# Decayed linear attention and a GELU MLP on one core: an earlier score block, a halved weight slice, and a shorter load lead

## The chip, the core and the metric

The kernel runs on one core of a Trainium2 chip. The metric is device time in microseconds (us) of one execution; for a comparison the medians of several executions are used. TensorE (PE) multiplies matrices, VectorE (DVE), ScalarE (ACT) and GpSimd (POOL) work elementwise, SyncE (SP) issues transfers. Each engine works through its own instructions in order and waits at semaphores for the others. GpSimd computes and also issues the loads that convert float32 to bf16.

## The reference

Inputs are q, k, v of 4 batches, 8 heads, 768 positions, 64 channels, a decay lam per head, and two weight matrices. Attention runs over blocks of positions with a state that decays:

```python
for b in range(nb):
    intra = np.einsum('bhic,bhjc->bhij', qb, kb) * Dmask[None]
    intra = np.einsum('bhij,bhjd->bhid', intra, vb)
    inter = np.einsum('bhid,bhde->bhie', qb * lam_pow[None], kv_state)
    out[:, :, sl] = intra + inter
    kb_dec = kb * rev_pow[None]
    kv_state = lam_block[None, :, None, None] * kv_state + np.einsum('bhsd,bhse->bhde', kb_dec, vb)
```

Its output, as 3072 rows of 512, goes through an MLP: h = x @ w_in (512 to 2048), g = h * (1 + erf(h / sqrt 2)) / 2, result = g @ w_out (2048 to 512), in float32.

## The kernel before

Positions are cut into 24 chunks of 128 (six for each batch), and four chunks make a group of 512 rows. Attention of a chunk gives a slice of x, transposed; when a group's x is full, its MLP follows: 16 column blocks of the first matmul (mm1, L288, each ended by a GELU on ScalarE, L290), then four output tiles of the second (mm2, L300).

One chunk's attention consists of these steps:

- begin: takes its loaded q, k, v.
- decay_k (L157): k scaled for the state, k_dec. On GpSimd, except in the first two chunks.
- transposes (L169): for chunks 0 to 7, on TensorE, emptied by ScalarE (kT) and VectorE (qT, with the decay). dma_transposes (L185): for chunks 8 to 23 both are transposes by transfers from SyncE; q is scaled on GpSimd first (q_hat, L190).
- scores (L193): eight matmuls into two PSUM tiles, two masking multiplications on VectorE. The PSUM tag has two buffers.
- next_state (L204): the product of k_dec and v is added to the state.
- outputs (L249): the state part (L253 or L259) and the score part (L263) in one PSUM tile o_ps, of which there is only one buffer; empty_outputs (L269) copies it to x, on ScalarE for chunks 0 to 7.

The order is written by hand and kept. The start (L371 to L397) interleaves chunks 0 to 3, with matmuls on an idle tile (keep_warm, L356) between them. GpSimd issues the loads of chunks 0 to 3 first (L76), then slice 0 of w_in (L381; a slice is a quarter of the columns, 512 of 2048), scales k of chunks 2 and 3, and then issues the other three slices of w_in, four slices of w_out (L399 to L402) and the loads of chunks 4 and on (L409 to L420). Transfers from GpSimd run on one queue in the order of issue. They use eight semaphores in turn, so that an issue waits until the eighth transfer before it has landed.

During the MLP of group 0, chunks 4 to 7 are worked in by a table of block numbers (group0, L425): at block 22 the transposes of chunk 4, and so on. Chunks 8 to 23 have due times: a list of steps sorted by the amount of matmul work done (L438 to L444), from which step (L446) is called between MLP blocks. A step of kind 0 begins chunk n: it issues kT's transfer on SyncE, q_hat on GpSimd, qT's transfer on SyncE, k_dec on GpSimd, and then, by prefetch (L342), all loads up to chunk n + 3 that are not issued yet. When chunk 8 begins, loads up to chunk 9 have been issued.

Of the kernel before, what the change touches and what calls it, by code (L numbers as in the profile page):

```python
# [15 lines left out]
def kernel(  # L16
# [10 lines left out]
    nc = tc.nc  # L27

    B, H, S, D = q.shape
    d_model, d_ff = moe_w_in.shape  # L30
# [9 lines left out]
    M = 4  # L40
# [22 lines left out]
    def load(n, name):  # L63
        raw[n, name] = qkv_pool.tile([128, H, D], BF16, tag=name, name=f"{name}_t")
        nc.gpsimd.dma_start(raw[n, name], chunk_of(name, n))  # L65
# [13 lines left out]
    w_in_t = w_pool.tile([128, NK1, d_ff], BF16)  # L79
    w_out_t = w_pool.tile([128, NK2, d_model], BF16)  # L80
    w_in_r = moe_w_in.rearrange("(ko ki) f -> ki ko f", ki=128)
    w_out_r = moe_w_out.rearrange("(ko ki) f -> ki ko f", ki=128)
    NS = 4

    def load_w_in(s):
        f = d_ff // NS
        nc.gpsimd.dma_start(w_in_t[:, :, s * f:(s + 1) * f], w_in_r[:, :, s * f:(s + 1) * f])

    def load_w_out(s):
        f = NK2 // NS  # L90
        nc.gpsimd.dma_start(w_out_t[:, s * f:(s + 1) * f, :], w_out_r[:, s * f:(s + 1) * f, :])
# [40 lines left out]
    def make_lam_blk():  # L132
        for hi in range(2):
            p = slice(hi * D, (hi + 1) * D)
            nc.vector.tensor_copy(lam_blk[p, :, p], lam_c_b[p])
# [9 lines left out]
    xT = {}  # L145
    states = {}

    def bank(shape, dtype, tag, name):
        return ps.tile(shape, dtype, tag=tag, name=name, bufs=2 if tag in ("sc", "mh", "mo") else 1)

    def begin(n, early=False):
        c = Chunk()
        c.n, c.sb, c.early = n, n % NB, early
        c.q, c.k, c.v = (raw.pop((n, name)) for name in "qkv")
        return c
# [29 lines left out]
    def dma_transposes(c):  # L185
        c.kT = work_pool.tile([128, HP, C], BF16, tag="kT", name="kT")
        c.qT = work_pool.tile([128, HP, C], BF16, tag="qT", name="qT")
        q_hat = work_pool.tile([128, H, D], BF16, tag="qh", name="q_hat")
        nc.sync.dma_start_transpose(out=c.kT, in_=c.k.rearrange("p h d -> p (h d)"))
        nc.gpsimd.tensor_mul(q_hat, c.q, lam_p[:, :, None].to_broadcast((128, H, D)))  # L190
        nc.sync.dma_start_transpose(out=c.qT, in_=q_hat.rearrange("p h d -> p (h d)"))

    def scores(c):  # L193
        sc_ps = [bank([128, HP, C], F32, "sc", f"sc_ps{hi}") for hi in range(2)]
        for hp in range(HP):
            for hi in range(2):
                p = slice(hi * D, (hi + 1) * D)
                nc.tensor.matmul(sc_ps[hi][:, hp, :], c.kT[p, hp, :], c.qT[p, hp, :], start=True, stop=True)  # L198
        c.sc_m = work_pool.tile([128, HP, 2, C], BF16, tag="sc_m", name="sc_m")
        dmask_r = dmask.rearrange("p (hp hi) i -> p hp hi i", hi=2)  # L200
        for hi in range(2):
            nc.vector.tensor_mul(c.sc_m[:, :, hi, :], sc_ps[hi], dmask_r[:, :, hi, :])  # L202

    def next_state(c):  # L204
        if c.sb == NB - 1:
            return
        if not c.early:
            return next_state_full(c)
        kv_ps = bank([128, HP, D], F32, "t", "kv_ps")
        for hp in range(HP):  # L210
            for hi in range(2):
                h = 2 * hp + hi
                nc.tensor.matmul(kv_ps[hi * D:(hi + 1) * D, hp, :], c.k_dec[:, h, :], c.v[:, h, :],
                                 start=True, stop=True)
        if c.n == M - 1:
            for hi in range(2):
                p = slice(hi * D, (hi + 1) * D)
                nc.vector.tensor_add(first_blk[p, :, p], kv_ps[p], states[c.n][1][p])
            states[c.n + 1] = first_blk, None
            return  # L220
        new = work_pool.tile([128, HP, D], BF16, tag="state", name="state")
        if c.sb == 0:
            nc.vector.tensor_copy(new, kv_ps)
        else:
            nc.vector.tensor_add(new, kv_ps, states[c.n][1])
        old = work_pool.tile([128, HP, D], F32, tag="old", name="old")
        states[c.n + 1] = new, old

    def decay_state(c):
        new, old = states[c.n + 1]  # L230
        for hp in range(HP):
            nc.scalar.activation(old[:, hp, :], new[:, hp, :], ACT.Copy, scale=lam_c[:, hp:hp + 1])

    def next_state_full(c):

        kv_ps = bank([128, HP, 128], F32, "t", "kv_ps")
        for hp in range(HP):
            nc.tensor.matmul(kv_ps[:, hp, :], c.k_dec[:, 2 * hp:2 * hp + 2, :], c.v[:, 2 * hp:2 * hp + 2, :],  # L238
                             start=True, stop=True)
        new = work_pool.tile([128, HP, 128], BF16, tag="state_f", name="state")  # L240
        if c.sb == 0:
            nc.vector.tensor_mul(new, kv_ps, lam_blk)
        else:
            tmp = work_pool.tile([128, HP, 128], F32, tag="tmp", name="tmp")
            nc.vector.tensor_add(tmp, kv_ps, states[c.n][0])  # L245
            nc.vector.tensor_mul(new, tmp, lam_blk)  # L246
        states[c.n + 1] = new, None

    def outputs(c, x_t, off, evacuate=True):  # L249
        o_ps = bank([128, HP, C], F32, "o", "o_ps")  # L250
        if c.sb > 0 and not c.early:
            for hp in range(HP):
                nc.tensor.matmul(o_ps[:, hp, :], states[c.n][0][:, hp, :], c.qT[:, hp, :],  # L253
                                 start=(hp == 0), stop=False, skip_group_check=True)
        elif c.sb > 0:
            for hp in range(HP):
                for hi in range(2):
                    p = slice(hi * D, (hi + 1) * D)
                    nc.tensor.matmul(o_ps[p, hp, :], states[c.n][0][p, hp, :], c.qT[p, hp, :],  # L259
                                     start=(hp == 0), stop=False, skip_group_check=True)  # L260
        for hp in range(HP):
            for hi in range(2):
                nc.tensor.matmul(o_ps[hi * D:(hi + 1) * D, hp, :], c.v[:, 2 * hp + hi, :], c.sc_m[:, hp, hi, :],  # L263
                                 start=(c.sb == 0 and hp == 0), stop=True, skip_group_check=True)
        c.x_o, c.o_ps = x_t[:, :, off * C:(off + 1) * C], o_ps
        if evacuate:
            empty_outputs(c)

    def empty_outputs(c):  # L269
        if c.n < 2 * M:  # L270
            nc.scalar.copy(c.x_o, c.o_ps)
        else:
            nc.vector.tensor_copy(c.x_o, c.o_ps)  # L273
# [68 lines left out]
    def prefetch(upto):  # L342
        while next_load[0] <= min(upto, NCH - 1):
            for name in "kqv":
                load(next_load[0], name)
            next_load[0] += 1
# [3 lines left out]
    live = {}  # L350
# [5 lines left out]
    def keep_warm(n, new=True):  # L356

        if new:
            idle_ps[0] = bank([128, 512], F32, "mo", "idle_ps")
        for _ in range(n):  # L360
            nc.tensor.matmul(idle_ps[0], idle[:, :128], idle, start=True, stop=True)  # L361

    def early(s, between=lambda: None):
        live[s] = begin(s, early=True)
        if s == 1:
            decay_k(live[s], nc.vector)
        transposes(live[s], between)
        if s != 1:
            decay_k(live[s], nc.scalar if s == 0 else nc.gpsimd)
# [9 lines left out]
    outputs(live[0], xT[0], 0, evacuate=False)  # L379
    scores(live[1])  # L380
    load_w_in(0)  # L381
    keep_warm(1)
    early(2)
# [1 line left out]
    next_state(live[1])  # L385
    scores(live[2])
    decay_state(live[1])
    outputs(live[1], xT[0], 1, evacuate=False)
    keep_warm(1)
    early(3)  # L390
    empty_outputs(live[1])
    next_state(live[2])
    outputs(live[2], xT[0], 2)
    scores(live[3])
    keep_warm(4)
    outputs(live[3], xT[0], 3)
    decay_state(live[2])  # L397
    make_lam_blk()
    for s in range(1, NS):  # L399
        load_w_in(s)  # L400
    for s in range(NS):
        load_w_out(s)  # L402
# [43 lines left out]
    def step(minus_kind, n):  # L446
        kind = -minus_kind
        g = n // M - 1
        if kind == 0:
            live[n] = begin(n)  # L450
            dma_transposes(live[n])
            decay_k(live[n], nc.gpsimd)
            prefetch(n + 3)
        elif kind == 2:
            scores(live[n])
            next_state(live[n])
        else:
            outputs(live[n], xT[g + 1], n % M)
# [46 lines left out]
```

## Time and profile before

| | |
|---|---|
| median of 5 runs | 217.72 us (217.07 to 219.0) |
| the profiled execution | 218.01 us, its span 216.2 us |
| TensorE busy | 204.9 us (95% of the span) |
| GpSimd busy | 105.3 us |
| first mm1 matmul starts | 19.50 us |
| transposes of chunk 4 (block 22 of group 0) | 38.87 us |
| scores of chunk 8, of chunk 9 | 56.46 us, 65.47 us |

All times in the profile are counted from the span's start. The page lists busy time by engine, the span in 40 slices, the chain of work that ended last, and groups of instructions with what ended the idle time before them. TensorE's idle time is 11.3 us in all: 1.2 before its first matmul, some 4 in the start up to 20 us, and pieces before single instructions later.

### The profile page before, as it was taken

The numbers are of one execution on the slowest core, as the hardware profiler recorded it, in microseconds if no ns is written. First come the engines' busy times: TensorE is split into PE (matmuls) and PEld (weight loads), VectorE is DVE, ScalarE is ACT, GpSimd is POOL, SyncE is SP. The second block draws the span as 40 slices with busy tenths as digits, with TensorE's granted clock in tenths as the row PEclk, the third lists the DMA queues.
The fourth block names the chain that finished last, engine by engine and source line by source line (L and its number), as shares of the span: only waits on it lengthen the run. The fifth ranks groups of instructions, "written<-read, shape, count | busy, mean of one in ns | idle before, by whom it ended". The sixth has DMA issues, their size and how long they took to land.

```text
span 216.2 us, 3545 instructions
## 1 busy us (share of the span) xinstructions
PE 204.9 (95%) x1422; PEld 102.9 (48%) x1446; DVE 73.4 (34%) x120; ACT 91.1 (42%) x169; POOL 105.3 (49%) x120
## 2 busy tenths in 40 slices
PE   7769999999998999999999999999999999999993
PEld 2345444555444545445545444545445545444452
DVE  4895000378515323406415413405415413100000
ACT  6975672334564221465221465221465221566121
POOL 8998333998999999467940819213000000000000
PEclk9999999999999999999999999999999999999999
DMA  6999999999999999999998697514351012100112
GB/s 40 146 158 195 200 207 185 155 209 137 189 142 125 165 147 163 200 125 96 112 125 150 78 164 64 36 69 127 75 98 24 3 70 75 50 0 3 49 49 97
DMA packets 100272, 24.35 MB, mean 113 GB/s; under 512 B 92960, under 2 KB 97312, under 8 KB 100256
## 3 DMA queue, kind: packets, MB, share of 16 engines
q0 software_dynamic: 79104, 13.64, 84.4%
q1 hardware_dynamic: 21152, 10.50, 22.7%
q8 instruction: 11, 0.18, 0.3%
q14 instruction: 5, 0.04, 0.1%
HBM read 27.27 MB, written 6.29 MB: 155 GB/s over the span
## 4 chain that ended last, share of the span: by engine, by line
PE 70%; DMA 14%; POOL 12%; issue 2%; ACT 0%; POOLq 0%
PE o_ps L300 32%; PE h_ps L288 28%; DMA q_t<-in_q_dram 8%; DMA w_in_t<-in_moe_w_in_dram 3%; POOL q_t L65 3%; POOL k_t L65 3%; POOL v_t L65 3%; DMA qT<-q_hat 3%; PE o_ps L263 3%; PE sc_ps L198 2%; POOL k_dec L167 2%; PE kv_ps L238 2%; PE o_ps L315 2%; PE o_ps L253 1%; POOL q_hat L190 1%
## 5 line engine op out<-in xcount | busy, mean ns | idle before, releaser
L288 PE MATMUL h_ps<-x_t,w_in_t 128*128 128x512 bf16 (+2 forms) x378 | 84.8, 377 | 1.0 <-DMA w_in_t<-in_moe_w_in_dram 0.5
L300 PE MATMUL o_ps<-w_out_t,g_t 128*128 128x512 bf16 x355 | 81.8, 379 | 0.8 <-issue 0.3
L290 ACT ACTIVATE g_t<-h_ps 128x512 bf16<-128x512 f32 x96 | 57.3, 597 | 33.9 <-PE h_ps L288 33.9
L288 PEld LDWEIGHTS <-w_in_t 128*128 128x128 bf16 x388 | 37.3, 98 | 43.8 <-DMA w_in_t<-in_moe_w_in_dram 0.6
L300 PEld LDWEIGHTS <-g_t 128*128 128x128 bf16 x368 | 34.7, 98 | 39.6
L305 ACT COPY o_sb<-o_ps 128x512 f32<-128x512 f32 x23 | 13.5, 586 | 68.3 <-PE o_ps L300 65.4
L273 DVE CAST x_t<-o_ps 128x512 bf16<-128x512 f32 x16 | 11.1, 692 | 73.0 <-PE o_ps L263 73.0
L202 DVE TENSOR_TENSOR sc_m<-sc_ps,dmask 128x512 bf16<-128x512 f32 x48 | 30.8, 683 | 14.7 <-PE sc_ps L198 14.4
L190 POOL TENSOR_TENSOR q_hat<-q_t,lam_p 128x512 bf16<-128x512 bf16 x16 | 16.9, 1057 | 18.1 <-DMA qT<-q_hat 17.3
L167 POOL TENSOR_TENSOR k_dec<-k_t,lam_m 128x512 bf16<-128x512 bf16 x16 | 17.2, 1077 | 15.0 <-PE kv_ps L238 9.1
L65 POOL DMA_DIRECT2D k_t<-in_k_dram x24 | 22.1, 921 | 3.7 <-DMA w_out_t<-in_moe_w_out_dram 1.7
L65 POOL DMA_DIRECT2D q_t<-in_q_dram x24 | 21.5, 896 | 4.8 <-DMA w_out_t<-in_moe_w_out_dram 3.4
L65 POOL DMA_DIRECT2D v_t<-in_v_dram x24 | 21.4, 894 | 3.3 <-DMA w_in_t<-in_moe_w_in_dram 1.7
L198 PE MATMUL sc_ps<-qT,kT 64*128 64x128 bf16 x192 | 9.5, 218 | 2.7 <-DVE qT L183 1.5
L183 DVE TENSOR_TENSOR qT<-t_ps,lam_q 128x512 bf16<-128x512 bf16 x8 | 5.5, 688 | 19.0 <-PE t_ps L174 18.8
L246 DVE TENSOR_TENSOR state<-tmp,lam_blk 128x512 bf16<-128x512 f32 x13 | 10.5, 808 | 0.5
L263 PE MATMUL o_ps<-sc_m,v_t 128*64 128x128 bf16 x192 | 10.1, 225 | 0.0
L198 PEld LDWEIGHTS <-kT 64*128 64x128 bf16 x192 | 5.7, 94 | 7.2 <-issue 3.6
L361 PE MATMUL idle_ps<-idle 128*128 128x512 bf16 x21 | 7.6, 476 | 1.2 <-DVE idle L94 1.2
L245 DVE TENSOR_TENSOR tmp<-kv_ps,state 128x512 f32<-128x512 f32 x12 | 8.2, 681 | 0.0
L180 ACT COPY kT<-t_ps 128x512 bf16<-128x512 bf16 x7 | 4.1, 579 | 9.4 <-PE t_ps L174 9.4
L263 PEld LDWEIGHTS <-v_t 128*64 128x64 bf16 x192 | 6.2, 109 | 3.3 <-issue 0.8
(57 smaller groups left out, 83.0 us busy)
## 6 DMA issues: line engine op xcount, KB each, us to landing
out_dram<-o_sb SPq DMA_DIRECT2D x23, 256.0 KB, 2.4
k_t<-in_k_dram POOLq DMA_DIRECT2D x24, 128.0 KB, 4.7
q_t<-in_q_dram POOLq DMA_DIRECT2D x24, 128.0 KB, 5.7
v_t<-in_v_dram POOLq DMA_DIRECT2D x24, 128.0 KB, 5.7
w_in_t<-in_moe_w_in_dram POOLq DMA_DIRECT2D x4, 512.0 KB, 8.3
w_out_t<-in_moe_w_out_dram POOLq DMA_DIRECT2D x4, 512.0 KB, 15.5
kT<-k_t SPq DMA_TRANSPOSE x16, 4.8
qT<-q_hat SPq DMA_TRANSPOSE x16, 4.1
```

The costliest lines, as they stand in the source:

```text
L65: nc.gpsimd.dma_start(raw[n, name], chunk_of(name, n))
L167: eng.tensor_mul(c.k_dec, c.k, scale[:, :, None].to_broadcast((128, H, D)))
L190: nc.gpsimd.tensor_mul(q_hat, c.q, lam_p[:, :, None].to_broadcast((128, H, D)))
L198: nc.tensor.matmul(sc_ps[hi][:, hp, :], c.kT[p, hp, :], c.qT[p, hp, :], start=True, stop=True)
L202: nc.vector.tensor_mul(c.sc_m[:, :, hi, :], sc_ps[hi], dmask_r[:, :, hi, :])
L246: nc.vector.tensor_mul(new, tmp, lam_blk)
L263: nc.tensor.matmul(o_ps[hi * D:(hi + 1) * D, hp, :], c.v[:, 2 * hp + hi, :], c.sc_m[:, hp, hi, :], start=(c.sb == 0 and hp == 0), stop=Tru ...
L273: nc.vector.tensor_copy(c.x_o, c.o_ps)
L288: nc.tensor.matmul(h_ps[:, lo:hi], w_in_t[:, ki, kf * 128:(kf + 1) * 128], x_t[:, ki, lo:hi], start=(ki == 0 and lo == 0), stop=(ki == NK1 ...
L290: nc.scalar.activation(g_t[:, kf, :], h_ps, ACT.Gelu)
L300: nc.tensor.matmul(om[io], g_t[:, kf, io * C:(io + 1) * C], w_out_t[:, kf, :], start=(kf == 0), stop=(kf == NK2 - 1))
L305: nc.scalar.copy(o_sb, om[io])
```

## The change

It has four edits.

- In the start, outputs of chunk 1 are emptied to x at once, and no longer after the transposes of chunk 3; scores of chunk 3 are put ahead of outputs of chunk 2; of four idle matmuls after them, two stay.
- Slice 0 of w_in is cut in two halves of 256 columns. The first is loaded where slice 0 was; the second is the first of those loaded after the start. The other slices are as before.
- prefetch of a kind 0 step loads up to n + 2 in place of n + 3.
- It does so only for chunks after 8: the step of chunk 8 issues no loads.

In the built order of GpSimd, q_hat and k_dec of chunk 9 follow those of chunk 8 directly, and the six loads of chunks 10 and 11 come after them. SyncE's order is unchanged.

```diff
     NS = 4
+    w_in_cuts = [0, 256, 512, 1024, 1536, 2048]

     def load_w_in(s):
-        f = d_ff // NS
-        nc.gpsimd.dma_start(w_in_t[:, :, s * f:(s + 1) * f], w_in_r[:, :, s * f:(s + 1) * f])
+        f = slice(w_in_cuts[s], w_in_cuts[s + 1])
+        nc.gpsimd.dma_start(w_in_t[:, :, f], w_in_r[:, :, f])
...
     scores(live[2])
     decay_state(live[1])
-    outputs(live[1], xT[0], 1, evacuate=False)
+    outputs(live[1], xT[0], 1)
     keep_warm(1)
     early(3)
-    empty_outputs(live[1])
     next_state(live[2])
+    scores(live[3])
     outputs(live[2], xT[0], 2)
-    scores(live[3])
-    keep_warm(4)
+    keep_warm(2)
     outputs(live[3], xT[0], 3)
     decay_state(live[2])
     make_lam_blk()
-    for s in range(1, NS):
+    for s in range(1, len(w_in_cuts) - 1):
         load_w_in(s)
...
             decay_k(live[n], nc.gpsimd)
-            prefetch(n + 3)
+            if n > 2 * M:
+                prefetch(n + 2)
```

## The prediction

> **What bounds the kernel now.** I read the page, then the chain of work that ended last, then TensorE's and GpSimd's timelines around the places the chain names.
>
> The page: TensorE is busy nearly all the time, at full granted clock in every slice, so only its idle time can be won.
>
> ```profile
> span 216.2 us, 3545 instructions
> PE 204.9 (95%) x1422; PEld 102.9 (48%) x1446; DVE 73.4 (34%) x120; ACT 91.1 (42%) x169; POOL 105.3 (49%) x120
> PEclk9999999999999999999999999999999999999999
> ```
>
> The chain (start, length, what) shows which work had to be waited for. From 14.73 to 39.27 it is not TensorE but transfers; from 44 to 65 GpSimd; then TensorE almost without a break.
>
> ```profile
> 14.73 7.25 DMA w_in_t<-in_moe_w_in_dram
> 22.27 17.01 DMA q_t<-in_q_dram
> 39.32 0.40 PE t_ps L174 x4
> ...
> 51.20 1.04 POOL q_hat L190
> 52.23 1.00 POOL k_dec L167
> 53.23 0.87 POOL k_t L65
> ...
> 57.62 0.87 POOL v_t L65
> 58.49 1.08 POOL q_hat L190
> 59.59 5.75 DMA qT<-q_hat
> 65.47 0.40 PE sc_ps L198 x8
> ```
>
> TensorE's timeline gives the idle time that belongs to these places (start, length, instructions, idle before and its releaser): 0.69 us before outputs of chunk 2, 0.48 us before the first w_in matmul, 0.37 and 0.81 us before scores of chunks 8 and 9. After 65.47 its idle pieces are 0.05 to 0.16 us each.
>
> ```profile
> 16.18 0.41 PE L259 MATMUL o_ps<-qT,state 64*64 64x128 bf16 x8 [0.69 <-ACT x_t L271]
> 19.50 1.05 PE L288 MATMUL h_ps<-x_t,w_in_t 128*128 128x384 bf16 x8 [0.48 <-DMA w_in_t<-in_moe_w_in_dram]
> 39.32 0.40 PE L174 MATMUL t_ps<-ident,q_t 128*128 128x128 bf16 x4
> 56.46 0.40 PE L198 MATMUL sc_ps<-qT,kT 64*128 64x128 bf16 x8 [0.37 <-DMA qT<-q_hat]
> 65.47 0.40 PE L198 MATMUL sc_ps<-qT,kT 64*128 64x128 bf16 x8 [0.81 <-DMA qT<-q_hat]
> ```
>
> GpSimd's timeline shows that its queue of transfers is full early: from 22 to 38 each load waits for an older weight slice to land.
>
> ```profile
> 22.27 0.88 POOL L65 DMA_DIRECT2D q_t<-in_q_dram  x1 [1.35 <-DMA w_in_t<-in_moe_w_in_dram]
> 24.81 0.87 POOL L65 DMA_DIRECT2D v_t<-in_v_dram  x1 [1.66 <-DMA w_in_t<-in_moe_w_in_dram]
> 37.69 0.87 POOL L65 DMA_DIRECT2D q_t<-in_q_dram  x1 [1.65 <-DMA w_out_t<-in_moe_w_out_dram]
> ```
>
> Loads released at 22.27 and 37.69 have six slices between them: 2.57 us a slice of 512 KB, 204 GB/s, which is the rate of the windows from 20 to 35 (200 to 206 GB/s). So weights, then chunk 4, stream back to back, and q of chunk 4 lands at 39.27 (22.27 + 17.01) because of the bytes ahead of it. TensorE reaches its transpose at that very moment (39.32, less than 0.1 us idle). This decides most of what follows.
>
> **Part 1, the order in the start.** Emptying outputs of chunk 1 at once puts its ScalarE copy (0.59) behind the state decay that ends at 14.76, so at 14.76 to 15.35; kT of chunk 3 goes behind it and ends at about 15.85 (15.65 before). qT of chunk 3 on VectorE ends at 15.97 as before, so scores of chunk 3 start at about 16.0: an idle 0.55 us in place of 0.69. Its masks on VectorE (1.29) then end near 17.75 instead of 18.59. Outputs of chunk 2 (two parts, 0.68) run to 17.1, two idle matmuls (0.43) lie under the copy of chunk 2 (0.59, to 17.75), outputs of chunk 3 (0.68) end at 18.4. Two idle matmuls fewer are part of this and cost nothing. Group 0's first matmul can start at 18.4 instead of 19.50, if its slice is there: half of slice 0 is 262 KB, at the 188 GB/s of the window from 15 to 20 1.4 us less than the whole, which TensorE got at 19.50; so about 18.1. Gain at this place 1.1 us.
>
> It is lost again. TensorE's queue is in order; after 1.1 us less it comes to the transposes of chunk 4 at about 37.8 and stands for k and q of chunk 4, q not before 39.27. In between no slice is late: the third and fourth column blocks want the second half at about 20.5 (it lands near 19.5), block 4 wants the next slice at 22.2 (21.98 before), later ones have 0.8 us and more. **Net 0**, and any delay of the weight stream, call it d, is paid in full at 39.3 and carried through q of chunk 8 and its transpose to 56.46. Nothing in the wait at 39.3 can make it cheaper: mm2 blocks are queued behind it.
>
> **Part 2, the halved slice.** Same bytes, one more issue on GpSimd (0.80 to 0.85 us; it lies at 14.7 to 20.7, when GpSimd next only waits for older slices, so 0). Two costs to the stream:
> - A hole. The first half is issued at 11.97 as before, starts when v of chunk 3 is through (the DMA share falls from 2.37 to 1.21 between 13 and 15, so about 14.5) and is through 1.4 us later, 15.9 to 16.1. The second half is issued at 14.73, behind two scalings of k. The first load, issued at 1.39, shows bytes from about 3.1 on (3 GB/s in the window 2 to 3, 67 in 3 to 4): 1.7 us. So its bytes start at 16.4: 0.3 us of hole. Bounds 0 (the lead is shorter in a warm queue) and 0.6.
> - Smaller packets. A w_in packet goes from 1024 to 512 bytes. Loads of q, k, v move 128-byte packets at 150 to 154 GB/s, 1024-byte ones go at 204: per engine 13.6 and 80 ns. On a line between them 512 bytes take 42, so 64 packets 2.70 us instead of 2.57: +0.13. Bounds: 0 (by bytes), and +0.9 at the rate of 128-byte packets (0.524 MB at 152 GB/s). I take 0.1, as 512 is nearer to 1024 in the line's terms.
>
> Sum **d = +0.4**, from 0 to 1.5.
>
> The Trainium skill has a rule against this edit: "DMA: Bandwidth & Descriptors", Anatomy of one DMA, gives each GpSimd transfer a fixed part of about 2.0 us beside its bytes. The rows above leave no room for it while transfers are queued: 2.57 us a slice is what 204 GB/s makes of its bytes alone. Were the 2.0 us paid for the extra transfer, the sum below would be +1.6 instead of -0.4 us, an estimate by that page, and the time 219.3.
>
> **Part 3, loads one chunk less ahead.** Before, six loads stand between scaling k of chunk 8 and q of chunk 9 on GpSimd: 53.19 to 58.49, 5.3 us (6 x 0.88). They go behind q_hat and k_dec of chunk 9. q of chunk 9 was issued at 48.72 and the neighbouring loads land within 6 us, so q_hat(9) runs at about 53.2 to 54.3, 5.3 us sooner. On SyncE's queue the order stays: two output stores (53.50, 55.06), kT(9) at 55.49, qT(9). That one waited for q_hat until 59.59; now it goes at 56.8, when kT(9)'s 1.3 us are over: 2.8 us sooner. It landed 5.75 us after issue; so at 62.6, against 64.66 when TensorE wants it (65.47 - 0.81). The 0.81 us go. Transposes beside loads took from 4.1 to 7.9 us to land in this stretch (kT(9) itself 7.9), at the worst 64.7: still in time.
>
> What is late next? k, q, v of chunks 10 and 11 are issued 2.1 us later (two operations, 1.04 + 1.03). k(10) landed about 58.4, then about 60.5; SyncE's kT(10) was issued at 60.89 and stays. q_hat(10) comes nearer, not later, since three loads of chunk 12 no longer stand before it. Scores of chunk 10 start at 73.68 and its transposes were issued by 64.74: room. From chunk 12 on GpSimd waits for its q_hat buffers anyway (17.3 us idle in four such waits), and loads two chunks ahead are still some 15 us ahead. No cost. The 0.37 us before scores of chunk 8 hang on q of chunk 8, which GpSimd waits 0.71 us for before q_hat at 51.20; all the order up to there is unchanged, so they stay. Bounds of part 3: -0.81 - 0.37 = -1.18, if fewer loads beside qT(8) let it land sooner, and 0, if qT(9) is late all the same.
>
> **Sum.** 0 + 0.4 - 0.81 = -0.4 us. The profiled run took 218.01 (216.2 span and 1.8 around it), 0.29 over the median 217.72; idle time won there is taken one for one. **217.3 us.** The five runs spread from 217.07 to 219.0, so 0.5% (1.1 us) is about what can be told from no change; this forecast is within it.
>
> **Rivals.**
> - *A: both transpose waits go and the stream is not delayed.* -1.18, 216.5. For: from 53.2 to 55.3 GpSimd's six loads no longer compete with qT(8), which was 0.24 to 0.37 us late. Against: its delay comes from before 53, and the hole in the stream.
> - *B: small packets are priced by the packet.* Place: the two half slices, 14.5 to 19. If a 512-byte packet took the 80 ns of a 1024-byte one, d is 2.57 + 0.3 = 2.9, and the time 217.72 + 2.9 - 0.81 = 219.8: slower. It decides from d = 1.9 on, that is 65 ns a packet. Against: 128-byte packets take 13.6.
> - *C: the edit does not free qT(9)*, because its transfer is held by the moved loads (now issued from 55.3 to 60.6, right beside it). It needs over 7.8 us from issue to landing; 7.9 has been seen once, beside more traffic. Then only d is left: +0.4, 218.1.
>
> **How the numbers follow.** Forecast case 0.48, A 0.25, B 0.12, C 0.15. With about 0.4 us of spread of a median: faster by over 0.5% needs -1.09, which A gives in six of ten and the forecast case in one of ten, 0.21. Slower needs +1.09: B nearly always, C in one of ten with d at its bound, 0.15 with a little for what I do not see. Within: 0.64. The range reaches from A with its spread (216.3) to C with d near 1.2 (218.9); B and tails are left out.
>
> **What would show it.** Right: first w_in matmul near 18.4 with no DMA wait; then TensorE idle about 1.2 to 1.6 us just before 39.3 to 39.7, released by k and q of chunk 4; q_hat(9) right behind k_dec(8); scores of chunk 9 without a wait; scores of chunk 8 still waiting. The start of chunk 4's q transposes, against 39.32, is d. Wrong: that start before 39.2 or after 40.8, a DMA wait at scores of chunk 9, or new waits of TensorE after 66.

## The result and the profile after

The changed kernel takes 218.92 us (median of 43 runs, 217.94 to 222.67); the kernel before, run beside it, 218.0 us (80 runs). The ratio is 1.0035, 95% interval [1.002, 1.005]: about 0.76 us slower. The forecast was 217.3 us, 0.4 us faster, with a range from 216.3 to 218.9. On the scale that it started from, the measured ratio gives 218.5 (217.72 x 1.0035), inside that range; the plain median of 218.92 lies just above its upper end. On either scale the kernel became slower, where the forecast had it faster.

The profiled execution of after took 219.94 us, its span is 218.1, that is 1.9 us more than the span of before. It is a longer execution than the median one, so it shows places better than sizes. Some executions here are over 1.5% longer than the fastest of their kernel; the ratios leave them out, and as the profiled ones of e6 and e17 are of that kind, only the first 40 us of e6 are read and nothing of e17. The start of e18's profile ran at half clock for 3.4 us. Head of the page:

```profile
span 218.1 us, 3547 instructions
PE 204.5 (94%) x1420; PEld 102.5 (47%) x1444; DVE 73.9 (34%) x120; ACT 90.9 (42%) x169; POOL 106.2 (49%) x121
PEclk9999999999999999999999999999999999999999
```

TensorE is as busy as before (204.5 and 204.9 us) at full clock: the 1.9 us are idle time. The chain of work that ended last (start, length, what) says whose:

```profile
15.50 8.20 DMA w_in_t<-in_moe_w_in_dram
23.99 16.88 DMA q_t<-in_q_dram
...
50.29 0.89 POOL q_t L65
52.06 1.67 issue
53.77 1.04 POOL q_hat L191
54.83 4.26 DMA qT<-q_hat
```

It is the same chain, weights and then q of chunk 4, with one difference: its first transfer is now the slice that follows the two halves, issued at 15.50 and landed at 23.70. Further down it no longer passes through the scores of chunk 9 but through q of chunk 8: what the chain calls "issue" at 52.06 is a wait for that load in GpSimd's own timeline.

```profile
53.77 1.04 POOL L191 TENSOR_TENSOR q_hat<-q_t,lam_p 128x512 bf16<-128x512 bf16 x1 [1.71 <-DMA q_t<-in_q_dram]
```

TensorE's timeline at the places that the forecast named (start, length, instructions, idle before and its releaser):

```profile
18.25 1.13 PE L289 MATMUL h_ps<-x_t,w_in_t 128*128 128x384 bf16 x8
...
23.75 2.55 PE L289 MATMUL h_ps<-x_t,w_in_t 128*128 128x512 bf16 x10 [1.43 <-DMA w_in_t<-in_moe_w_in_dram]
...
39.95 0.40 PE L175 MATMUL t_ps<-ident,k_t 128*128 128x128 bf16 x4 [0.49 <-DMA k_t<-in_k_dram]
40.91 0.40 PE L175 MATMUL t_ps<-ident,q_t 128*128 128x128 bf16 x4 [0.56 <-DMA q_t<-in_q_dram]
...
59.23 0.40 PE L199 MATMUL sc_ps<-qT,kT 64*128 64x128 bf16 x8 [1.55 <-DMA qT<-q_hat]
...
67.36 0.40 PE L199 MATMUL sc_ps<-qT,kT 64*128 64x128 bf16 x8
```

The first w_in matmul starts at 18.25, without a wait, 1.25 us sooner than before. All of that and more is idle again by 40.91, where 39.32 stood before. Then the wait at the scores of chunk 8 has grown from 0.37 to 1.55 us, and that at the scores of chunk 9 is gone. From the scores of chunk 9 to the end of the span both kernels take 150.7 us. So the whole difference of the two profiles is in three numbers: +1.59 up to chunk 4, +1.18 from there to chunk 8, and -0.88 from chunk 8 to chunk 9; together +1.89.

### The profile page after: what moved, and what is told of

Its sections match the earlier page's. It is cut to its first block, busy times and chain, and to the rows that moved or that the text cites. A ratio compares the mean times of both kernels' runs of the same rounds, so it can differ in the third digit from the quotient of the medians.

```text
span 218.1 us, 3547 instructions
## 1 busy us (share of the span) xinstructions
PE 204.5 (94%) x1420; PEld 102.5 (47%) x1444; DVE 73.9 (34%) x120; ACT 90.9 (42%) x169; POOL 106.2 (49%) x121
## 4 chain that ended last, share of the span: by engine, by line
PE 74%; DMA 13%; POOL 8%; issue 2%; ACT 0%; POOLq 0%
PE o_ps L301 32%; PE h_ps L289 31%; DMA q_t<-in_q_dram 8%; DMA w_in_t<-in_moe_w_in_dram 4%; PE sc_ps L199 3%; PE o_ps L264 3%; POOL k_t L65 2%; PE kv_ps L239 2%; POOL q_t L65 2%; DMA qT<-q_hat 2%; POOL v_t L65 2%; PE o_ps L316 2%; PE o_ps L254 2%; POOL k_dec L168 1%; POOL w_in_t L88 1%
## 5 line engine op out<-in xcount | busy, mean ns | idle before, releaser
L247 DVE TENSOR_TENSOR state<-tmp,lam_blk 128x512 bf16<-128x512 f32 x13 | 11.0, 845 | 0.4
L362 PE MATMUL idle_ps<-idle 128*128 128x512 bf16 x19 | 6.7, 470 | 1.2 <-DVE idle L95 1.2
```

## The experiments

All are compared with the kernel before, run beside them. Three places are read from each profile: the start of chunk 4's q transposes ("q4"), which is the weight stream's clock, and the starts of the scores of chunks 8 and 9, with the wait before each in brackets.

| run | ratio to before, 95% | q4 | scores 8 | scores 9 |
|---|---|---|---|---|
| before | | 39.32 | 56.46 (0.37) | 65.47 (0.81) |
| e11, before again | | 39.60 | 56.76 (0.39) | 64.90 (0) |
| after | 1.0035 [1.0020, 1.0050] | 40.91 | 59.23 (1.55) | 67.36 (0) |
| e12, after again | | 41.65 | 59.61 (1.19) | 67.75 (0) |
| e1, order and lead | 0.9995 [0.9964, 1.0026] | 38.85 | 56.21 (0.58) | 64.34 (0) |
| e2, halves | 1.0083 [1.0053, 1.0114] | 41.51 | 58.83 (0.55) | 66.97 (0) |
| e3, lead | 0.9995 [0.9961, 1.0029] | 39.76 | 56.89 (0.37) | 65.03 (0) |
| e4, order | 1.0004 [0.9973, 1.0035] | 39.56 | 57.16 (0.83) | 65.30 (0) |
| e17, halves and order | 1.0077 [1.0033, 1.0121] | | | |
| e18, halves and lead | 1.0013 [0.9971, 1.0055] | 40.98 | 58.02 (0.27) | 66.15 (0) |

### e1 to e4: each part away or alone

e1 is the changed kernel with slice 0 whole:

```diff
-    w_in_cuts = [0, 256, 512, 1024, 1536, 2048]
+    w_in_cuts = [0, 512, 1024, 1536, 2048]
```

> The changed kernel with slice 0 of w_in whole again. Theory S (the halved slice delays the weight stream, and through q of chunks 4 and 8 the scores of chunk 8; the shorter load lead is a gain): q transposes of chunk 4 start at 39.3 to 39.5 again, not 40.9; scores of chunk 8 at 56.5 with the old 0.4 us wait; scores of chunk 9 without a wait; time 0.8 us under the kernel before. Rival L (the shorter lead itself makes scores of chunk 8 late): scores of chunk 8 still wait 1 us or more and the time is 0 to 1 us over the kernel before. Rival O (the new order of the start slows the transfers): q of chunk 4 is still late by about 1 us.

Measured 217.85 us, 0.9995: no change against before, although both other edits are in; the 0.8 us expected of the shorter lead did not come. q4 is at 38.85, no later than in before.

e2 has only the halves, e3 only the shorter lead, e4 only the order of the start (each the hunk of the diff shown above).

> The kernel before with slice 0 of w_in in two halves, nothing else. Theory S: q transposes of chunk 4 start 1 to 1.6 us later than 39.3, scores of chunk 8 are 1.6 to 2.8 us later than 56.5, and the 0.8 us wait at scores of chunk 9 stays or shrinks; time 1.0 to 2 us over the kernel before. Rivals L and O: within 0.4 us of the kernel before.

Measured 219.65 us, 1.0083, which is 1.8 us: more than the whole change loses. q4 comes 2.2 us after before's.

```profile
24.15 1.04 PE L289 MATMUL h_ps<-x_t,w_in_t 128*128 128x512 bf16 x4 [1.06 <-DMA w_in_t<-in_moe_w_in_dram]
...
41.51 0.40 PE L175 MATMUL t_ps<-ident,q_t 128*128 128x128 bf16 x4 [0.56 <-DMA q_t<-in_q_dram]
```

These two lines of TensorE's timeline of e2 show the same two waits as after, at the slice behind the halves and at q of chunk 4. Taken out of the change, the halves take the loss with them (e1); put alone into the kernel before, they bring it (e2). So the halved slice is the cause of the slowdown.

> The kernel before with the shorter load lead, nothing else. Theory S: no wait at scores of chunk 9, the 0.4 us at scores of chunk 8 stay, 0.8 us under the kernel before. Rival L: scores of chunk 8 wait more than 1 us; the time is not under the kernel before.

Measured 218.13 us, 0.9995: the lead alone gains nothing in the median. Its profile shows no wait at chunk 9, and one further on (TensorE's timeline; line 198 is scores, here of chunk 12):

```profile
90.02 0.40 PE L198 MATMUL sc_ps<-qT,kT 64*128 64x128 bf16 x8 [0.64 <-DMA qT<-q_hat]
```

> The kernel before with the new order in the start, nothing else. Theory S: outputs of chunk 3 end near 18.3, the first w_in matmul still waits for slice 0 until about 19.5, q of chunk 4 lands at 39.3; within 0.3 us of the kernel before. Rival O: q of chunk 4 lands 0.5 us or more later and the time is that much over the kernel before.

Measured 218.18 us, 1.0004: nothing, as the forecast had it. And here, where loads still go three chunks ahead, the scores of chunk 9 don't wait either.

### e11 and e12: both kernels profiled again

> The kernel before, profiled a second time. If the 0.81 us wait at scores of chunk 9 is typical of it, waits of TensorE at scores of chunks 8 and 9 are again 1.0 to 1.3 us together. If it was a feature of that execution, they are 0.5 to 0.8 us together, and that is why taking it away gained less than 0.81 us in the medians.

> The changed kernel, profiled a second time. Theory S: last w_out slice again at 38.6 to 39.6, q transposes of chunk 4 at 40.5 to 41.5 after waits, no wait at scores of chunk 9. The 1.55 us at scores of chunk 8 are larger than in the kernel with halves alone (0.55); if that was that one execution's, 0.4 to 0.9 us stand there.

TensorE's timeline of e11:

```profile
56.76 0.40 PE L198 MATMUL sc_ps<-qT,kT 64*128 64x128 bf16 x8 [0.39 <-DMA qT<-q_hat]
...
64.90 0.40 PE L198 MATMUL sc_ps<-qT,kT 64*128 64x128 bf16 x8
```

The unchanged kernel has no wait at chunk 9 in this execution, which took 217.44 us in place of 218.01: qT of chunk 9 landed at 64.75, 0.15 us before it was wanted. So the 0.81 us on which the forecast's gain rested come in some executions and not in others. The other profiles agree. Of nine whose step of chunk 8 issues loads (before, e11, e2, e4, e5, e7, e13, e14, e15), two have a wait at the scores of chunk 9, 0.81 us in before and 2.61 us in e13; of nine without those loads (after, e12, e1, e3, e8, e9, e10, e16, e18), none has. e12 shows the late weights of after once more (q4 at 41.65), and the large wait at chunk 8 (1.19).

### e5, e6, e7: the hole or the small packets

e5 issues both halves ahead of the two k scalings, so that nothing lies between them. e6 leaves slice 0 whole and halves the last slice of w_in, deep in a full queue: the same small packets, no hole. e7 cuts slice 0 into two halves of its rows, so that its packets stay at 1024 bytes, with the hole as in the change.

```diff
 e5:
     load_w_in(0)
+    load_w_in(1)
 ...
-    for s in range(1, len(w_in_cuts) - 1):
+    for s in range(2, len(w_in_cuts) - 1):
 e6:
-    w_in_cuts = [0, 256, 512, 1024, 1536, 2048]
+    w_in_cuts = [0, 512, 1024, 1536, 1792, 2048]
 e7:
+    def load_w_in_rows(half):
+        r = slice(half * (NK1 // 2), (half + 1) * (NK1 // 2))
+        nc.gpsimd.dma_start(w_in_t[:, r, :d_ff // NS], w_in_r[:, r, :d_ff // NS])
 ...
-    load_w_in(0)
+    load_w_in_rows(0)
 ...
+    load_w_in_rows(1)
     for s in range(1, NS):
         load_w_in(s)
```

> The kernel before with slice 0 in two halves, both issued at the place of slice 0, ahead of the two scalings of k; so the queue does not run dry between them, but the packets are as small as in the change. With whole slices the last w_out slice landed at 36.9 to 37.8 in four kernels, with halves at 38.9 and 39.6. Theory H (the hole between the halves costs it): last w_out slice lands at 37 to 38, time within 0.5 us of the kernel before or below. Theory P (512-byte packets or one more transfer cost it): 38.9 or later, and 1 to 2 us over the kernel before.

> The kernel before with the last slice of w_in in two halves in place of the first; at that point the queue is full, so there is no hole. Theory H: last w_out slice lands at 37 to 38, same time as before. Theory P: 38.9 or later, 1 to 2 us over.

> The kernel before with slice 0 in two transfers of half the rows each (k blocks 0 and 1, then 2 and 3) in place of half the columns: packets keep 1024 bytes, the second is issued behind the two scalings of k. The same hole without small packets. Theory H: last w_out slice lands at 38.6 or later, 1 to 2 us over the kernel before. Theory P: 37 to 38.2, within 0.5 us.

| run | packets of the halves | between the halves on GpSimd | last w_out slice landed | ratio |
|---|---|---|---|---|
| before / e11 | no halves | | 37.41 / 37.67 | |
| e6 | 512 B | nothing, queue full | 37.43 | 1.0028 [0.9976, 1.0079] |
| e5 | 512 B | nothing | 38.28 | 1.0033 [1.0006, 1.0059] |
| e7 | 1024 B | two k scalings | 38.98 | 1.0104 [1.0058, 1.0150] |
| e2 | 512 B | two k scalings | 39.55 | 1.0083 [1.0053, 1.0114] |

The ratio of e7 rests on four runs. The landing of the last slice scatters by itself: in the other kernels with slice 0 whole and no pause (e1, e3, e4, e8, e9, e10) it lies between 36.90 and 37.83. e6 is within that. Its two halves land at 25.56 and 26.88, 2.67 us after the slice ahead of them (24.21), where a whole slice takes 2.5 to 2.6. So 512-byte packets cost about 0.1 us at most where transfers are queued (the ratio of e6 is inconclusive). e7 has large packets and loses 1.3 to 1.6 us of stream. So the size of the packets is not the cause; the place of the second half, behind the two scalings, is most of it (0.7 us from e5 to e7, 1.3 from e5 to e2). e5 lies between, 0.6 to 0.9 us late with nothing between the halves. What it shares with the change is the extra issue, which puts the next slice on the queue 0.7 to 0.8 us later; e14 below delays that slice by 1.0 us in another way.

### e13 to e15: how much a gap costs

Why should a hole of nominally 0.3 us cost 1.6? e13 puts the second half between the two scalings, so that by the issue times there is no gap. e14 and e15 leave slice 0 whole and put one or two spare multiplications on GpSimd, of 1.04 us each, before the other slices; their results are used by nothing, so the computation is unchanged.

```diff
 e13 (to e2):
     keep_warm(1)
     early(2)
+    load_w_in(1)
 ...
-    for s in range(1, len(w_in_cuts) - 1):
+    for s in range(2, len(w_in_cuts) - 1):
 e14, e15 (to before; 1 and 2 times):
+    for _ in range(2):
+        spare = work_pool.tile([128, H, D], BF16, tag="spare", name="spare")
+        nc.gpsimd.tensor_mul(spare, live[3].k, lam_k[:, :, None].to_broadcast((128, H, D)))
     for s in range(1, NS):
         load_w_in(s)
```

> The kernel before with the first w_in slice halved, and the second half issued between the two k scalings (first half, k scaling of chunk 2, second half, k scaling of chunk 3, the other slices). In e2, where both k scalings lie between the halves, the last w_out slice landed at 39.55 and q4 at 41.47; in the kernel before at 37.41 and 39.27. By the issue times the second half is asked for at about 13.7 and its bytes can flow about 1.6 us later, at 15.3, before the first half is through (about 15.9), so there is no gap between them. Theory 'nominal gap' (the stream loses what the queue stands empty): last w_out slice at 37 to 38, q4 at 39 to 40, time 0.998 to 1.002 of before. Theory 'thin queue' (a queue with little in it loses several times the gap): the half is only 0.5 MB and the slices behind it come after another k scaling, so last w_out slice at 38.3 to 39.5, q4 at 40.2 to 41.5, time 1.003 to 1.009.

> The kernel before, its first w_in slice whole, with one spare multiplication on GpSimd (1.04 us, its result is not used, the computation is unchanged) after the two k scalings, so that all later weight slices are issued about 1.04 us later. The whole slice keeps the queue in work until about 17.6; the next slice can flow from about 17.4: no gap. Theory 'nominal gap': last w_out slice at 37.3 to 37.9, q4 at 39.2 to 39.8, time 0.998 to 1.002. Theory 'thin queue': last w_out slice at 38.0 to 39.0, time 1.002 to 1.006.

> As the run with one spare multiplication, but with two (2.08 us), the results unused and the computation unchanged. The next slice can flow from about 18.5, the first is through at about 17.6: a gap of 0.9 us. Theory 'nominal gap': last w_out slice 0.9 us later than in the kernel before, at 38.3 to 38.6, q4 at 40.2 to 40.5, time 1.003 to 1.005. Theory 'thin queue': two to four times that, last w_out slice at 39.2 to 41, q4 at 41 to 43, time 1.008 to 1.016.

| run | last w_out slice landed | q4 | ratio |
|---|---|---|---|
| e13 | 37.84 | 39.81 | 1.0044 [1.0000, 1.0087] |
| e14 | 38.42 | 40.34 | 1.0063 [1.0034, 1.0093] |
| e15 | 38.78 | 40.75 | 1.0084 [1.0053, 1.0115] |

The ratio of e15 rests on four runs. e13 is what "nominal gap" expected of the stream: 0.2 to 0.4 us later than the two profiles of before, at the edge of the scatter. Its time, 1.0044, is not; that is in the range of "thin queue". Six of its ten times are at 217.9 to 218.7; in the other four, the profiled one among them, it took 219.2 to 221.1, and that profile has 2.61 us of idle time at the scores of chunk 9. By the last slice e14 fits "thin queue" (0.75 to 1.0 us for a pause that should have been free), and e15 lies between its theories (1.1 to 1.4 us).

But the last slice doesn't say where a delay arose. The table has the landings of four slices; each shows in GpSimd's timeline as the end of a load's wait, some 0.3 us later.

| run | next whole slice of w_in | first w_out slice | second | last |
|---|---|---|---|---|
| before | 21.98 | 29.74 | 32.27 | 37.41 |
| e11 | 22.37 | 30.00 | 32.54 | 37.67 |
| after | 23.70 | 31.31 | 33.86 | 38.93 |
| e2 | 24.11 | 31.75 | 34.54 | 39.55 |
| e7 | 23.33 | 30.98 | 34.27 | 38.98 |
| e5 | 22.86 | 30.43 | 33.08 | 38.28 |
| e13 | 22.04 | 29.61 | 32.77 | 37.84 |
| e14 | 22.48 | 30.23 | 33.59 | 38.42 |
| e15 | 22.20 | 29.83 | 33.57 | 38.78 |

In after and e2 the whole loss, 1.3 to 2.1 us, stands at the next whole slice, and from there on the slices follow each other about as before. There the halves with two scalings between them cost 0.5 to 1.3 us more than the halves together (e7, after and e2 against e5). e15, with the longest gap, has that slice within 0.2 us of before, and the three behind it about as close; it is late only from the second w_out slice on (GpSimd's timeline of e15; the second row starts when that slice has landed):

```profile
30.12 0.87 POOL L65 DMA_DIRECT2D q_t<-in_q_dram  x1 [1.67 <-DMA w_out_t<-in_moe_w_out_dram]
33.85 0.87 POOL L65 DMA_DIRECT2D v_t<-in_v_dram  x1 [2.86 <-DMA w_out_t<-in_moe_w_out_dram]
```

In e14, too, 0.1 to 0.5 us stand at the next slice and the rest arises between these two. Why a slice some 15 us behind the pause takes 3.4 to 3.7 us instead of 2.5 isn't shown. So the profiles of e14 and e15 don't show what a gap costs; their medians (1.0063 and 1.0084) say that the pauses make the kernel slower, not by which way.

The windows of 1 us tell more. Columns: window, its length, busy PE, PEld, DVE, ACT and POOL with counts, granted clock, DMA share, GB/s. First the kernel before:

```profile
16.00:17.00 1.00, 0.82 (x22) 0.63 (x23) 0.31 (x1) 0.15 (x2) 1.00 (x3) 1.00 1.20 188
17.00:18.00 1.00, 0.95 (x11) 0.40 (x8) 0.70 (x2) 0.57 (x1) 1.00 (x3) 1.00 1.09 176
18.00:19.00 1.00, 1.00 (x18) 0.58 (x16) 0.99 (x3) 0.00 (x0) 1.00 (x2) 1.00 1.24 190
19.00:20.00 1.00, 0.52 (x5) 0.31 (x4) 0.40 (x1) 0.94 (x3) 1.00 (x3) 1.00 1.21 200
20.00:21.00 1.00, 1.00 (x17) 0.67 (x15) 0.09 (x1) 1.00 (x4) 0.92 (x2) 1.00 1.25 207
21.00:22.00 1.00, 1.00 (x6) 0.45 (x5) 0.76 (x2) 0.38 (x2) 0.00 (x0) 1.00 1.25 209
```

After, the same windows:

```profile
16.00:17.00 1.00, 1.00 (x25) 0.64 (x20) 0.90 (x3) 0.07 (x1) 1.00 (x3) 1.00 1.01 142
17.00:18.00 1.00, 0.64 (x13) 0.45 (x14) 0.99 (x3) 0.51 (x1) 1.00 (x3) 1.00 1.35 174
18.00:19.00 1.00, 1.00 (x13) 0.56 (x14) 0.21 (x1) 0.64 (x2) 1.00 (x2) 1.00 1.00 141
19.00:20.00 1.00, 1.00 (x16) 0.62 (x14) 0.07 (x1) 1.00 (x5) 1.00 (x3) 1.00 1.10 170
20.00:21.00 1.00, 1.00 (x6) 0.48 (x5) 0.78 (x2) 0.75 (x2) 1.00 (x3) 1.00 1.14 169
21.00:22.00 1.00, 1.00 (x7) 0.39 (x4) 0.00 (x0) 0.73 (x2) 0.65 (x1) 1.00 1.20 183
```

e15, whose queue was empty for longest:

```profile
17.00:18.00 1.00, 1.00 (x12) 0.38 (x8) 0.72 (x2) 0.55 (x1) 1.00 (x2) 1.00 0.85 145
18.00:19.00 1.00, 1.00 (x18) 0.58 (x16) 0.99 (x3) 0.00 (x0) 1.00 (x2) 1.00 0.45 51
19.00:20.00 1.00, 0.46 (x4) 0.31 (x4) 0.16 (x1) 0.95 (x3) 1.00 (x3) 1.00 1.14 185
20.00:21.00 1.00, 1.00 (x16) 0.62 (x14) 0.04 (x1) 0.95 (x4) 1.00 (x2) 1.00 1.25 205
```

In after the hole itself is as the forecast had it: 46 GB/s are missing from 16 to 17, which is 46 KB, or 0.22 us at 205 GB/s. In windows of 0.2 us the rate is 74 GB/s from 16.2 to 16.4 and 182 from 16.6 on, so the second half, issued at 14.72, is there 1.7 to 1.9 us later (1.7 in the forecast). But from 18 to 22 the stream runs at 141 to 183 GB/s in place of 190 to 209, with four and more slices issued behind the half. Those four windows miss 143 KB, 0.70 us. That is the part the forecast didn't have. e2 has 98, 130, 167 and 167 GB/s there; e7, cut by rows, is slow from 15 on (128, 123, 145 and 113, then 177, 198 and 205).

These sums are sizes of what is seen, not a full account of the 1.3 to 1.5 us: a rate adds up all transfers under way, and a slice has landed only with its last packet. The four windows of e15 miss 187 KB against before, 0.9 us, and its next slice still landed on time. What holds the stream down behind the half slice, the profile doesn't show. It is not what VectorE does meanwhile: its instructions lie in e2 within 0.2 us of where they lie in before (the masks of chunk 3 start at 17.37 and 17.30), and still e2 has the slower stream.

### e16: q of chunk 8

In the two profiles of after, q of chunk 8 lands 1.90 and 1.73 us after k of that chunk, in the other profiles above 0.7 to 1.6. The list of transfers of after from 50.9 to 52.3 (queue, kind: packets, MB, share of 16 engines) holds a load of instructions on top:

```profile
q0 software_dynamic: 1454, 0.18, 208.6%
q8 instruction: 1, 0.02, 4.3%
```

One packet of 16 KB, 0.96 us long, starts at 51.1 in after, and at 51.8 in e12. In before it starts at 48.3. e16 is the changed kernel with four idle matmuls in place of two:

```diff
-    keep_warm(2)
+    keep_warm(4)
```

> The changed kernel with four idle matmuls ahead of the first chunk's outputs instead of two, as in the kernel before: four more instructions on TensorE's list. The halved slice stays, so the last w_out slice lands at 38.9 to 39.7 and q4 at 40.9 to 41.7 either way. Theory 'instruction fetch': the 16 KB load of instructions that fell on the tail of q of chunk 8's load (51.1 and 51.8 in the two profiles of the changed kernel) is tied to the place in the list, so it moves by about 0.5 us or less; if it leaves the load of q of chunk 8, q lands 0.8 to 1.4 us after k of that chunk (1.73 and 1.90 in the changed kernel), the wait at the scores of chunk 8 falls from 1.55 and 1.19 to 0.4 to 0.8, and the time is 0.996 to 0.999 of the changed kernel (1.000 to 1.002 of before). Theory 'late weights alone': q lands 1.7 to 1.9 after k, the wait stays at 1.2 to 1.5, time 1.003 to 1.005 of before. The two idle matmuls in themselves lie in TensorE's start, ahead of a wait for weights, and cost 0 to 0.2 us.

Measured 218.93 us, 1.0041 [1.0018, 1.0064]: as the changed kernel, so the two idle matmuls are worth nothing. In its profile the packet is at 50.1, q of chunk 8 lands 0.87 us behind k, and TensorE's timeline has

```profile
41.14 0.40 PE L175 MATMUL t_ps<-ident,q_t 128*128 128x128 bf16 x4 [0.56 <-DMA q_t<-in_q_dram]
...
58.13 0.40 PE L199 MATMUL sc_ps<-qT,kT 64*128 64x128 bf16 x8 [0.22 <-DMA qT<-q_hat]
```

with weights as late as in after, but 1.1 us less at chunk 8. The profile agrees with the theory of the instruction load; the median, unmoved, doesn't: whatever q of chunk 8 lost in the two profiles of after is not what the typical run loses. And e15 has q 1.59 us behind k and a wait of 1.21 at chunk 8 with its packet at 50.1. Not settled.

The Trainium skill, "Runtime: NRT & Kernel Launch", Instruction fetch mechanics, says that instructions are fetched in blocks of 16 KiB on a queue of their own, and that this is mostly hidden. The size agrees with the packets here (16 KB, 0.9 to 1.0 us); whether one was not hidden behind q of chunk 8 is what e16 leaves open.

### e17 and e18: which part gives back 1 us

The halves alone lose 1.8 us, the whole change 0.8, and the two other parts alone are worth nothing. e17 adds only the order to the halves, e18 only the lead (hunks as in the change).

> The kernel before with the halved slice and the changed order of the start, loads still three chunks ahead. The halves alone measured 1.0083 of before (1.0053 to 1.0114), the whole change 1.0035 (1.0020 to 1.0050); so order and shorter lead together give back about 1 us where the weights come late, though each alone gave nothing where they come in time (1.0004 and 0.9995). Theory 'lead gives it back' (less is loaded beside the transposes that the scores of chunks 8 and 9 wait for): 1.007 to 1.010 here. Theory 'order gives it back': 1.002 to 1.005 here. Either way the last w_out slice at 38.9 to 39.7.

> The kernel before with the halved slice and loads two chunks ahead, order of the start unchanged. Theory 'lead gives it back': 1.002 to 1.005 of before, with no wait or one below 0.3 us at the scores of chunk 9. Theory 'order gives it back': 1.007 to 1.010. If both runs come out at 1.003 to 1.006, the halves alone were measured too high, and nothing needs giving back.

Measured 219.92 us, 1.0077 with the order, and 218.89 us, 1.0013 with the lead. The halves cost about 0.8% with loads three chunks ahead (e2, e17) and 0.1 to 0.4% with two (e18, after). The intervals of e17 and e18 overlap, those of e2 and after don't. So the shorter lead does give back about 1 us, but only where the weights come late. Its place isn't shown: e2's profile, with the long lead, has no wait at the scores of chunk 9 to remove. A wait there in some executions only, as in e13, is a candidate that no run tests.

### e8 to e10: a version without the halves

> The changed kernel with slice 0 whole and the lead of three chunks kept, but no loads in the step of chunk 8; so chunks 10 to 12 are loaded after q of chunk 9 is scaled, and later chunks as in the kernel before. Scores of chunk 9 without a wait. If the shorter lead is what let the scores of chunk 12 wait in the run with the lead alone (0.64 us at 90.0), that wait is gone and the time 0.5 to 1.0 us under the kernel before; if it comes from TensorE being earlier there, it stays, and the time is within 0.4 us of the kernel before.

e8 has the order and the skipped loads of chunk 8's step, but the old lead after that; 217.47 us, 0.999 [0.9972, 1.0009]. Its scores of chunk 12 don't wait; but neither do those of e1, which has the short lead, so the 0.64 us of e3 don't tell of the lead.

```diff
 e8 (to before, with the order of the change):
-            prefetch(n + 3)
+            if n > 2 * M:
+                prefetch(n + 3)
```

e9 moves the loads of k and q of chunk 8 ahead of v of chunk 7; e10 also issues the second whole slice of w_in before the k scalings.

```diff
 e9 (to e8):
-  (7, "q"), (7, "v"), (8, "k")]
+  (7, "q"), (8, "k"), (8, "q")]
 ...
-  [(8, "q"), (8, "v")]
+  [(7, "v"), (8, "v")]
 e10 (to e9):
     load_w_in(0)
+    load_w_in(1)
 ...
-    for s in range(1, NS):
+    for s in range(2, NS):
```

> The kernel with the new order of the start, slice 0 whole, lead of three chunks, no loads in the step of chunk 8; and q and k of chunk 8 loaded ahead of v of chunk 7. Theory S (scores of chunk 8 hang on q of chunk 8 in GpSimd's load queue): q of chunk 8 lands about 1 us sooner (49.9 to 50.3, not 51.0 to 51.2), the 0.4 to 0.8 us wait at scores of chunk 8 goes, no wait at scores of chunk 9, and the time is 0.5 us or so under the kernel without this step, 0.7 to 1.2 us under the kernel before. Rival (that wait is set by SyncE's transposes beside the loads): it stays at 0.3 us or more.

> The same, with slices 0 and 1 of w_in both issued ahead of the two scalings of k. If a thin queue in the start is what slows the weight stream (184 to 190 GB/s from 15 to 19 us in the kernel before, 98 to 174 with the halves apart, 200 to 210 later), the stream is at 195 GB/s or more from 15 on and the last w_out slice lands at 36.6 to 37.0; time the same or 0.3 us less than without it. If the slow stretch has another cause (loads of chunk 3 ending unevenly), it lands at 37.2 to 37.8 as before.

e9: 217.64 us, 0.9970 [0.9942, 0.9998]. e10: 217.57 us, 0.9958 [0.9925, 0.9991], which is faster than before by its interval, if only by 0.9 us. Neither gains where it was meant to. The wait at the scores of chunk 8 stays, at 0.68 and 0.63 us (0.37 and 0.39 in the profiles of before). Line of e9's timeline:

```profile
56.95 0.40 PE L198 MATMUL sc_ps<-qT,kT 64*128 64x128 bf16 x8 [0.68 <-DMA qT<-q_hat]
```

q of chunk 8 landed 0.9 us sooner than in e8, at 50.08, as expected, but its transpose at 56.81, beside loads; the wait is at the transposes, not at the load. And in e10 the last w_out slice landed at 37.74, no sooner than before. Why their ratios are lower isn't shown; in microseconds they are no lower than e8 (217.47), and the kernel before had a median of 218.61 beside them, higher than beside the other runs.

## Why the prediction was wrong, point by point

- **The halved slice, d = +0.4 us: this is the step that failed.** Its line "Sum d = +0.4, from 0 to 1.5" measured 1.59 us by its own yardstick, the start of chunk 4's q transposes against 39.32 (2.33 in e12, 2.19 in e2), and 1.8 us in medians where it is the only edit (e2). By its terms: the smaller packets, 0.1, cost no more than that (e6). "One more issue on GpSimd", put at 0, brings the next whole slice to the queue 0.7 to 0.8 us later; in e5, which has the halves and this delay but nothing between the halves, that slice landed 0.5 to 0.9 us late. The hole, "0.3 us", bounds "0 (the lead is shorter in a warm queue) and 0.6", is there with its 0.2 to 0.3 us of missing bytes and with the lead of 1.7 us that the forecast took; but with it that slice landed another 0.5 to 1.3 us later (e7, after and e2 against e5). The forecast let the stream go on at full rate behind a hole, where it ran at 141 to 183 GB/s for four more microseconds. Why it did stays open. No row of before showed a queue that had nearly run dry in front of large transfers, so the bounds, taken from the gap's length, were too narrow.
- **The skill's rule.** "DMA: Bandwidth & Descriptors", Anatomy of one DMA, gives a fixed part of about 2.0 us to each GpSimd transfer. Where transfers are queued, no run shows it: e6 has one more transfer, and its two halves together took 2.67 us, 0.1 us more than a whole slice. For the slice that was cut in front, an estimate by that figure makes d 2.4 us (0.4 and 2.0); the measured 1.6 to 2.3 us in q4 are nearer to it than to 0.4. But e13 makes the same cut, with as many transfers, and loses 0.2 to 0.4 us of stream. So the place of the issue matters more than the count of transfers.
- **The order of the start, net 0: right.** The first w_in matmul was expected near 18.4 and came at 18.25 without a wait. The 1.1 us were to be lost again at the transposes of chunk 4; they were, and e4 measured 1.0004. That "in between no slice is late" was wrong: the slice behind the halves was late for block 4 by 1.43 us. TensorE would have waited at chunk 4 for the same stream, so by the order of its queue this wait adds nothing to the sum; no run tests that apart.
- **The shorter lead, -0.81 us: the forecast's reason did not hold.** The mechanism was as told: q_hat of chunk 9 ran at 55.92, right behind k_dec of chunk 8, its transpose was issued at 58.73, and the scores of chunk 9 didn't wait. But the wait was in one execution of before and not in the next (e11), and e3, with only this edit, measured 0.9995. The sum counted it as if every execution had it, while qT of chunk 9 lands 0.15 us before it is wanted in e11 and 0.68 us after that in the profile that was read. With the weights late, the edit did give back about 1 us (e2 and e17 against after and e18), by a way that was not shown.
- **"They stay": the 0.37 us at the scores of chunk 8.** They became 1.55 and 1.19 in the two profiles of after, 0.22 to 0.58 in the other runs with a cut slice 0 (e2, e5, e7, e13, e16, e18), and 1.21 in e15, where it is whole. So the forecast's statement holds for most, and the cause of the two large ones stays open.
- **The rivals.** A (no delay of the stream) fell with e2. B named the right edit and the right sign, by the wrong mechanism: small packets are not priced by the packet (at 80 ns each the halves of e6 would have taken about 5.1 us, and they took 2.67). C (the edit frees nothing) has the right value for the lead alone, but not its reason, since qT of chunk 9 was early.
- **The check on the numbers.** With the measured 1.8 for d in place of 0.4, the forecast's own sum is +1.0 us, and 0.76 was measured. One term was mis-sized, and it turned the sign. That the rest of the sum then fits is partly luck: it keeps -0.81 for the lead, which alone measured nothing (e3) and gave back about 1 us only beside the late weights, for a reason that the forecast did not have.

## What to carry to other kernels

Look at what an in-order issuing engine does between two transfers of a stream that sets the end: here two multiplications between the halves of one slice made the end of the stream 1.3 to 2.3 us late, while the same cut with one multiplication between (e13) or a cut deep in the queue (e6) made it 0 to 0.4. Don't price a gap in such a stream by its length alone; if a slice is to be cut for an early start, issue the pieces so that the next is in the queue before the first has drained, and even then none of the cuts here gained (e5, e13). To find where a delay arises, compare the landings of all the transfers, not only of the last. And a wait that is 0.8 us long in one profile is worth checking in a second execution before a gain is counted from it: compare when the transfer lands with when it is wanted.

## What the runs showed of the hardware

- After the gap between the two halves, the stream of weights ran at 98 to 183 GB/s from 18 to 22 us although four and more transfers were issued behind it (e2, after), and the next whole slice landed 1.3 to 2.1 us late; a full queue ran at 200 to 210 GB/s. A longer gap between whole slices (e15, 51 GB/s in its emptiest window) was followed by 185 and then 205 GB/s, and its next slice landed within 0.2 us of before's. Why the two differ is open.
- Two half slices of 512-byte packets in a full queue landed 2.67 us behind the slice ahead of them (e6); whole slices of 1024-byte packets follow each other in 2.5 to 2.6 us.
- Instructions are loaded beside the data, in packets of 16 KB that take 0.9 to 1.0 us each in the first 55 us; near chunk 8 they start at 48.3 us in before, 51.1 and 51.8 in the two profiles of after, 50.1 in e16.
